# Where the spread reciprocals of a linear attention lie, how they are written, and when their transfers are issued

## The chip, the cores and the metric

The kernel runs on one core of one Trainium2 chip. The metric is device time in microseconds (us) of one execution. A NeuronCore has the engines TensorE (PE: matmuls; its weight loads are listed apart as PEld), VectorE (DVE), ScalarE (ACT), GpSimd (POOL) and SyncE (SP, which here only issues DMAs). All times of day below are us from the start of the profiled span.

## What is computed

Four layers in turn on x of 2048 tokens by 576 features: linear attention (A), MLP (B), A, B, each with a layer norm before it and a residual after it.

```python
def _A_ref(x, wqkv, wo):            # H = 32 heads of Dh = 18
    ...
    pq, pk = phi(q), phi(k)
    kv = jnp.einsum("bhsd,bhse->bhde", pk, v)
    z = jnp.einsum("bhsd->bhd", pk)
    num = jnp.einsum("bhqd,bhde->bhqe", pq, kv)
    den = jnp.einsum("bhqd,bhd->bhq", pq, z)[..., None] + 1e-6
    o = num / den
    return (lambda x, *d: x.transpose(*d))(o, 0, 2, 1, 3).reshape(B, S, D) @ wo
def _B_ref(x, w1, b1, w2, b2):      # F = 4608
    y = _layernorm(x, axis=-1)
    h = _gelu(jnp.einsum("bsd,df->bsf", y, w1) + b1)
    return jnp.einsum("bsf,fd->bsd", h, w2) + b2
```

The change concerns the division by `den`: one value per head and token.

## The kernel before

The 2048 tokens are cut into 16 tiles of 128 and into 4 blocks of 512, counted 0 to 3 here as in the code (the change's title counts them from 1). `yT` holds the normed activations with features on partitions: 128 partitions x 5 feature chunks x 2048 tokens, so block `c` has the columns `c * 512` to `(c + 1) * 512`. The heads lie in five groups `g` of 7, 7, 7, 7 and 4 heads. Work is written out by hand: `pe`, `vec`, `act`, `pool` and `sp` keep each engine's instructions in the order of the program (L45 to L63), SP's DMAs too. Waits between engines come from the tiles that they read and write.

An attention layer (`layer_A`, L467) first runs over the tiles for keys and values, then forms `kvwo`, the product of each head's key-value matrix with the output weights, so that a tile's output is one chain of five matmuls on `pq`, the query features. `pq` lies in slots of `units`; group 4 of two blocks (0 and 1, or 2 and 3) shares one slot, block `c` in the partitions from `64 * (c % 2)` on (L534 to L536, `q_rows` L652). A matmul of group 4 reads all 128 partitions of that slot.

Before the outputs, `pq` is divided by the denominators. For each block:

- `den_stage(c)` (L661): 24 small matmuls on PE give the denominators as 128 partitions (32 heads x 4 tiles) x 128 tokens; DVE takes the reciprocal into `rden`. For blocks 1 to 3 SP writes it to `rden_rows[c]` in DRAM, 32 heads x 512 tokens, in four DMAs of 32 rows, one per tile (L672).
- `spread(c)` (L678): 7 DMAs read `rden_rows[c]` back with each head's row repeated 18 times, so that each partition of `pq` has its head's reciprocals beside it. They go into `spare(0)` to `spare(4)`, the five chunks of `yT` in block 1's columns, whichever block they are for. Groups 0 to 3 take one DMA each (126 partitions), a fifth fills partitions 126 and 127 for all four, two more serve group 4.
- `scales(c)` (L789): five multiplies on DVE, one per group, `pq = spare * pq`.
- `outputs(c)` (L798): `wo_stage` for the block's 4 tiles, ten matmuls each on PE, and the residual on DVE.

Block 0 goes another way (`quad_rden`, `scale_first`): its reciprocals are spread by matmuls. In between, `groups(n)` (L793) lets PE do `n` of the next MLP's first-matmul groups on block 0, which need nothing of this. The layer ends with (L802 to L815):

```python
            scales(1)
            groups(3)
            den_stage(2)
            den_stage(3)
            outputs(1)
            spread(2)
            scales(2)
            spread(3)
            scales(3)
            groups(3)
            outputs(2)
            outputs(3)
```

`outputs(1)` stands ahead of `spread(2)` in the program, but puts nothing on SP here: a residual is followed by a DMA in the last layer alone (L464). Since `spread(2)` and `spread(3)` write the same rows, each waits until DVE's multiplies have read the earlier block's. The columns of `yT` for blocks 1 to 3 are filled anew, with the MLP's normed rows, only while the MLP runs (`place_rows`, L396).

Of the kernel before, what the change touches and what calls it, by code (L numbers as in the profile page):

```python
# [8 lines left out]
ALU = mybir.AluOpType  # L9
# [5 lines left out]
S, D, F, H, DH = 2048, 576, 4608, 32, 18  # L15
P = 128
# [11 lines left out]
TPC = CB // P  # L28
CA = 512
# [6 lines left out]
def build(tc, A_x, A_wqkv, A_wo, B_w1, B_b1, B_w2, B_b2, out, n_layers=4):  # L36
    nc = tc.nc
    with ExitStack() as ctx:
# [23 lines left out]
        vec, act = InOrder(nc.vector, "VectorE"), InOrder(nc.scalar, "ScalarE")  # L62
        pool, sp = InOrder(nc.gpsimd, "GpSimd"), InOrder(nc.sync, "SyncE")  # L63
# [21 lines left out]
        def one(name, tag=None):  # L85
            return ps_one.tile([P, 512], F32, name=name, tag=tag or one_tag())
# [106 lines left out]
        yT = const.tile([P, KD, S], BF16, name="yT")  # L193
# [16 lines left out]
        rden_rows = [dpool.tile([H, CA], BF16, name=f"rden_rows{c}") for c in range(NCA)]  # L210
# [12 lines left out]
        def mm(out_, lhsT, rhs, start, stop, **kw):  # L223
            return pe(nc.tensor.matmul(out_, lhsT=lhsT, rhs=rhs, start=start, stop=stop, **kw))  # L224
# [242 lines left out]
        def layer_A(li, next_kind, begin, before_tile, before_keys, mid_tile, rows_ahead, after_tile, q_tiles, placed, mlp):  # L467
            es, pks, kps, vas, pq, ys = {}, {}, {}, {}, {}, {}
# [183 lines left out]
            def q_rows(g, c):  # L652
                return slice(64 * (c % 2), 64 * (c % 2) + 64) if g == 4 else slice(0, P)

            def spare(i):

                return yT[:, i, CA:2 * CA]

            quad_rden = spare(3)

            def den_stage(c):  # L661
                dp = one("den_ps", "one3" if c == 0 else None)
                for g in range(G + 1):
                    for j in range(TPC):
                        sel, by = (zsel[:, g + (g == 4 and c % 2), :], pq[(g, c)][:, j * P:(j + 1) * P]) if g < G else (eps_sel[:], ident[:])
                        mm(dp[32 * j:32 * (j + 1), 0:P], sel, by, g == 0, g == G)
                rden = work.tile([P, P], BF16, name="rden", bufs=2)
                with nc.allow_low_precision("reciprocal of the denominator in the reference's bfloat16"):
                    vec.reciprocal(out=rden[:], in_=dp[:, 0:P])
                if c > 0:  # L670

                    for j in range(TPC):  # L672
                        sp.dma_start(out=rden_rows[c][:, j * P:(j + 1) * P], in_=rden[32 * j:32 * (j + 1), :])
                    return
                vec.tensor_tensor(out=quad_rden.rearrange("p (j n) -> p j n", j=4), in0=quad_mask[:],
                                  in1=rden[:].unsqueeze(1).to_broadcast([P, 4, P]), op=ALU.mult)

            def spread(c):  # L678
                heads = rden_rows[c]
                for g in range(4):  # L680
                    sp.dma_start(out=spare(g)[0:126, :],
                                 in_=heads[7 * g:7 * g + 7, :].unsqueeze(1).to_broadcast([7, DH, CA]))
                sp.dma_start(out=yT[126:P, 0:4, CA:2 * CA],
                             in_=heads[31:32, :].unsqueeze(1).to_broadcast([2, 4, CA]))
                at = 64 * (c % 2)
                sp.dma_start(out=spare(4)[at:at + 54, :], in_=heads[28:31, :].unsqueeze(1).to_broadcast([3, DH, CA]))
                sp.dma_start(out=spare(4)[at + 54:at + 64, :], in_=heads[31:32, :].to_broadcast([10, CA]))

            def scale_stage(g, c):
                rows = q_rows(g, c)  # L690
                vec.tensor_tensor(out=pq[(g, c)][rows, :], in0=spare(g)[rows, :], in1=pq[(g, c)][rows, :], op=ALU.mult)

            def scale_first(half, tags):

# [9 lines left out]
            def wo_stage(t):  # L704
                c, j = divmod(t, TPC)
                wp = pair("wo_ps")
                for half in range(2):
                    for g in range(G):
                        by = kvwo[g] if g < 4 else kvwo[g][c % 2]
                        mm(wp[:, half, 0:HALF], pq[(g, c)][:, j * P:(j + 1) * P],  # L710
                           by[:, half * HALF:(half + 1) * HALF], g == 0, g == G - 1)
                residual(li, t, wp[:, :, 0:HALF])
# [7 lines left out]
                              in1=side[0:126, 0:260].rearrange("p (g c) -> p g c", g=4)[:, :, 64:65].to_broadcast([126, 4, H]),  # L720
                              op=ALU.mult)
            vec.tensor_copy(out=products[0:65, 4, 0:V4].rearrange("p (g d) -> p g d", g=4), in_=tp[0:65, :, 0:126])
            vec.tensor_copy(out=zk[96:P, :].rearrange("p (i c) -> p i c", i=2),
                            in_=side[96:P, 264:328].unsqueeze(1).to_broadcast([32, 2, 64]))
# [3 lines left out]
                                     in1=sums_sb[96:P, :], op0=ALU.mult, op1=ALU.add)  # L728
            vec.tensor_tensor(
                out=kvT[0:72, 4, 0:72].rearrange("p (h e) -> p h e", h=4),  # L730
                in0=side[0:72, 264:336].rearrange("p (h e) -> p h e", h=4),
                in1=maskz[0:72, 0:4, :], op=ALU.mult)
# [3 lines left out]
            for k in range(KD):  # L736
                rows = slice(0, P if k < 4 else 65)
                for g in range(4):
# [5 lines left out]
                              in1=zp[:, 0:1].unsqueeze(1).to_broadcast([P, 2, H]), op=ALU.mult)  # L744
            vec.tensor_tensor(
                out=kvT[0:126, 0:4, :].rearrange("p g (h e) -> p g h e", h=7),
                in0=kvp[0:126, 0:V4].rearrange("p (g h e) -> p g h e", g=4, h=7),
                in1=maskz[0:126, :, :].unsqueeze(1).to_broadcast([126, 4, 7, DH]), op=ALU.mult)
            kv_wo(4, act)
            q_next(True, "one0")  # L750
            finish(len(q_late) - 3)
            den_stage(0)
            kv_wo(0, act)
            kv_wo(1, act)
# [26 lines left out]
            q_next(True)  # L781
            first[3].transposed()
            den_stage(1)
            spread(1)
            warm_table(ACT.Gelu_apprx_tanh)
            assert not q_left


            def scales(c):  # L789
                for g in range(G):  # L790
                    scale_stage(g, c)
# [6 lines left out]
            def outputs(c):  # L798
                for t in range(c * TPC, (c + 1) * TPC):
                    wo_stage(t)  # L800

            finish(len(q_late))  # L802
            scales(1)
            groups(3)
            den_stage(2)
            den_stage(3)
            outputs(1)
            spread(2)
            scales(2)
            spread(3)  # L810
            scales(3)
            groups(3)
            outputs(2)
# [216 lines left out]
        for li, kind in enumerate(kinds):  # L1030
            nk = kinds[li + 1] if li + 1 < n_layers else None
            if kind == "A" and li == 0:
                layer_A(li, nk, begin0, before_tile0, before_keys0, mid_tile0, rows_ahead0, after_tile0, (1, 2, 3, 5, 7, 10, NT - 2), False,
                        mlps.get(li + 1))
            elif kind == "A":
                layer_A(li, nk, None, lambda t: lnq.tick(), nothing, nothing, nothing, lambda *a: None, range(4, 10), True,
                        mlps.get(li + 1))
            else:
                mlps[li].run()
# [48 lines left out]
```

## Time and profile before

| | |
|---|---|
| median of 3 runs | 757.26 us (755.1 to 758.77) |
| the profiled execution | 757.15 us, its span 755.4 us |
| TensorE busy | 745.9 us, 99% of the span |
| VectorE, ScalarE, GpSimd busy | 36%, 39%, 15% |
| mean granted TensorE clock | 0.998 |
| DMA | 34.48 MB; the SP and ACT hardware queue (q1) takes 16.9% of 16 engines |
| `rden_rows<-rden` | 24 DMAs of 8 KB, issue 412 ns (median) |
| `yT<-rden_rows` | 42 DMAs, 24 of 126 KB, 6 of 54, 6 of 10 and 6 of 8; issue 729 ns (median) |

How to read a profile row: `L224 PE MATMUL wo_ps<-shared,units ... x288 | 42.8, 294 | 3.7 <-DVE units` means 288 matmuls recorded on line 224 (the helper `mm`) that write `wo_ps`, 42.8 us busy, 294 ns each, and 3.7 us in which the engine stood idle just before one of them, ended by DVE's write of `units`. L53 is the helper that issues every DVE, ACT, POOL and SP instruction, so these are told apart by their tiles. In the chain of work that ended last, "issue" is time with no visible wait, and "SPq" is SP issuing a DMA; a row "DMA" runs from the start of a transfer's issue to its landing. "PEclk" or granted clock is the share of full speed that TensorE's clock was allowed.

### The profile page before, as it was taken

How to read it: one execution, taken by the hardware profiler on the slowest of the kernel's cores; microseconds unless marked ns; L12 is line 12 of the kernel's file. 1: busy time of each engine (PE TensorE's matmuls, PEld its weight loads, DVE VectorE, ACT ScalarE, POOL GpSimd, SP SyncE). 2: the span in 40 equal slices, each digit the busy share in tenths (PEclk: the TensorE clock that was granted, in tenths of full speed). 3: DMA queues.
4: the chain of work that ended last, by engine and by line, in shares of the span. 5: the costliest groups of instructions: out<-in, count | busy, mean ns of one | idle time of the engine just before them, and what ended most of it. 6: DMA issues, size and time to landing. Idle time of an engine off the chain costs nothing.

```text
span 755.4 us, 15366 instructions
## 1 busy us (share of the span) xinstructions
PE 745.9 (99%) x6423; PEld 469.2 (62%) x6438; DVE 268.5 (36%) x653; ACT 298.1 (39%) x652; POOL 114.5 (15%) x245
## 2 busy tenths in 40 slices
PE   9999989999999999999999999999999999999998
PEld 5666446774477457646776665557646754774476
DVE  7987644333223402500355576333310240100000
ACT  5656841205700750274035475440174037205700
POOL 4541100321111201200200020012210120010010
PEclk9999999999999999999999999999999999999999
DMA  7990120022011202110032001102000200020000
GB/s 206 270 355 20 35 68 1 2 56 46 2 18 42 44 2 36 37 32 1 18 109 67 2 10 42 60 1 39 29 2 1 51 17 1 11 49 10 1 9 25
DMA packets 60741, 34.48 MB, mean 46 GB/s; under 512 B 37088, under 2 KB 60672, under 8 KB 60672
## 3 DMA queue, kind: packets, MB, share of 16 engines
q1 hardware_dynamic: 59312, 32.94, 16.9%
q8 instruction: 50, 0.82, 0.5%
q10 hardware_dynamic: 1360, 0.56, 0.3%
q14 instruction: 19, 0.16, 0.1%
HBM read 21.70 MB, written 4.93 MB: 35 GB/s over the span
## 4 chain that ended last, share of the span: by engine, by line
PE 92%; DMA 2%; SPq 2%; DVE 2%; issue 1%; POOL 0%; ACT 0%; DVEq 0%
PE m_ps L224 37%; PE hp_ps L224 19%; PE h_ps L224 15%; PE k_ps L224 6%; PE q_ps L224 5%; PE wo_ps L224 4%; PE rk_ps L224 3%; SPq L53 2%; DMA yT<-rden_rows 1%; DVE units L53 1%; PE tp L383 1%; PE side_ps L224 1%; DMA wkv_sb<-in_A_wqkv_dram 1%; PE den_ps L224 0%; PE kvwo_ps L224 0%
## 5 line engine op out<-in xcount | busy, mean ns | idle before, releaser
L224 PEld LDWEIGHTS <-units 128*128 128x128 bf16 x2688 | 260.8, 98 | 79.6 <-issue 5.1
L224 PE MATMUL m_ps<-w_sb,units 128*128 128x288 bf16 (+2 forms) x2304 | 283.6, 286 | 0.0
L224 PEld LDWEIGHTS <-w_sb 64*128 64x128 bf16 x2304 | 123.9, 94 | 136.7 <-ACT relay_sb L53 4.1
L224 PE MATMUL h_ps<-yT,w_sb 64*128 64x512 bf16 x1152 | 178.0, 376 | 0.0
L224 PE MATMUL hp_ps<-yT,w_sb 64*128 64x512 bf16 x1152 | 148.0, 376 | 0.1
L53 DVE TENSOR_TENSOR x_sb<-m_ps,xo 128x576 bf16<-128x576 f32 (+2 forms) x33 | 24.4, 738 | 325.3 <-PE m_ps L224 325.3
L53 ACT COPY relay_sb<-relay_sb 128x1 f32<-128x1 f32 x144 | 27.7, 192 | 270.4 <-PE hp_ps L224 253.7
L53 ACT ACTIVATE units<-hp_ps,b1T 128x512 bf16<-128x512 f32 x144 | 91.0, 683 | 59.1 <-PE hp_ps L224 58.2
L53 POOL TENSOR_TENSOR xo<-x_sb,b_bc 128x576 f32<-128x576 bf16 x32 | 40.7, 1273 | 414.0 <-DVE x_sb L53 299.4
L53 ACT ACTIVATE units<-h_ps,b1T 128x512 bf16<-128x512 f32 x144 | 96.1, 687 | 0.0
L224 PE MATMUL hp_ps<-yT,w_tail 64*128 64x512 bf16 x144 | 54.1, 376 | 0.0
L224 PE MATMUL h_ps<-yT,w_tail 64*128 64x512 bf16 x144 | 54.1, 376 | 0.0
L224 PE MATMUL k_ps<-wkv_sb,yT 128*128 128x288 bf16 (+1 forms) x320 | 52.5, 301 | 0.4 <-DMA wkv_sb<-in_A_wqkv_dram 0.2
L53 DVE BATCH_NORM_STATS2 ln_st<-x_sb 128x6 f32<-128x288 bf16 x128 | 51.3, 440 | 1.0 <-DMA x_sb<-in_A_x_dram 0.7
L53 ACT ACTIVATE phi_e<-k_ps 128x288 bf16<-128x288 f32 x64 | 26.4, 413 | 52.1 <-PE k_ps L224 50.8
L53 ACT ACTIVATE units<-q_ps 128x512 bf16<-128x512 f32 x72 | 38.4, 596 | 21.4 <-PE q_ps L224 21.2
L53 DVE STREAM_TRANSPOSE shared<-y_ring 128x640 bf16<-128x640 bf16 x40 | 32.9, 826 | 39.0 <-DMA yT<-shared 30.2
L224 PE MATMUL wo_ps<-shared,units 128*128 128x288 bf16 x288 | 42.8, 294 | 3.7 <-DVE units L53 3.7
L53 DVE TENSOR_SCALAR y_ring<-x_sb,ln_mv,ln_rstd 128x576 bf16<-128x576 bf16 x57 | 30.9, 542 | 41.4 <-POOL ln_rstd L53 41.4
L224 PE MATMUL q_ps<-yT,wq_sb 128*128 128x512 bf16 (+1 forms) x185 | 43.1, 380 | 0.7
L224 PEld LDWEIGHTS <-w_tail 64*128 64x128 bf16 x288 | 27.1, 94 | 17.0
L224 PEld LDWEIGHTS <-yT 128*128 128x128 bf16 x320 | 30.4, 98 | 11.2 <-issue 0.9
(96 smaller groups left out, 425.7 us busy)
## 6 DMA issues: line engine op xcount, KB each, us to landing
yT<-shared SPq DMA_DIRECT2D x160, 40.0 KB
w_sb<-in_B_w_dram SPq DMA_DIRECT2D x12, 432.0 KB
w_sb<-in_B_w_dram SPq DMA_DIRECT2D x9, 512.0 KB
yT<-rden_rows SPq DMA_DIRECT2D x24, 126.0 KB
y_rows<-y_ring SPq DMA_DIRECT2D x16, 144.0 KB
units<-y_rows SPq DMA_DIRECT2D x16, 144.0 KB
x_sb<-in_A_x_dram SPq DMA_DIRECT2D x15, 144.0 KB
out_dram<-x_sb SPq DMA_DIRECT2D x15, 144.0 KB
```

Source lines behind the costliest of these rows:

```text
L53: inst = issue(*args, **kw)
L224: return pe(nc.tensor.matmul(out_, lhsT=lhsT, rhs=rhs, start=start, stop=stop, **kw))
L383: pe(nc.tensor.transpose(out=tp[:, k - a, :], in_=self.y[:, k * P:(k + 1) * P], identity=ident[:]))
```

## The change

Three things change. (1) `spare(c)` is now block `c`'s own columns of `yT`, so that each block's spread reciprocals have a place of their own. (2) Each block's reciprocals are written to `rden_rows[c]` in one DMA that covers all 128 partitions (seen from DRAM as 4 tiles x 32 heads x 128 tokens) in place of four. (3) `spread(2)` and `spread(3)` stand right behind `den_stage(3)`, ahead of `outputs(1)`. `quad_rden` keeps the place that it had.

```diff
-            def spare(i):
-
-                return yT[:, i, CA:2 * CA]
-
-            quad_rden = spare(3)
+            def spare(c):
+
+                return yT[:, :, c * CA:(c + 1) * CA]
+
+            quad_rden = spare(1)[:, 3, :]
...
-                    for j in range(TPC):
-                        sp.dma_start(out=rden_rows[c][:, j * P:(j + 1) * P], in_=rden[32 * j:32 * (j + 1), :])
+                    sp.dma_start(out=rden_rows[c].rearrange("h (j n) -> j h n", j=TPC), in_=rden[:])
...
             def spread(c):
-                heads = rden_rows[c]
+                heads, to = rden_rows[c], spare(c)
+                at = 64 * (c % 2)
                 for g in range(4):
-                    sp.dma_start(out=spare(g)[0:126, :],
-                                 in_=heads[7 * g:7 * g + 7, :].unsqueeze(1).to_broadcast([7, DH, CA]))
-                sp.dma_start(out=yT[126:P, 0:4, CA:2 * CA],
-                             in_=heads[31:32, :].unsqueeze(1).to_broadcast([2, 4, CA]))
-                at = 64 * (c % 2)
-                sp.dma_start(out=spare(4)[at:at + 54, :], in_=heads[28:31, :].unsqueeze(1).to_broadcast([3, DH, CA]))
-                sp.dma_start(out=spare(4)[at + 54:at + 64, :], in_=heads[31:32, :].to_broadcast([10, CA]))
+                    sp.dma_start(out=to[0:126, g, :], in_=heads[7 * g:7 * g + 7, :].unsqueeze(1).to_broadcast([7, DH, CA]))
+                sp.dma_start(out=to[126:P, 0:4, :], in_=heads[31:32, :].unsqueeze(1).to_broadcast([2, 4, CA]))
+                sp.dma_start(out=to[at:at + 54, 4, :], in_=heads[28:31, :].unsqueeze(1).to_broadcast([3, DH, CA]))
+                sp.dma_start(out=to[at + 54:at + 64, 4, :], in_=heads[31:32, :].to_broadcast([10, CA]))

             def scale_stage(g, c):
                 rows = q_rows(g, c)
-                vec.tensor_tensor(out=pq[(g, c)][rows, :], in0=spare(g)[rows, :], in1=pq[(g, c)][rows, :], op=ALU.mult)
+                vec.tensor_tensor(out=pq[(g, c)][rows, :], in0=spare(c)[rows, g, :], in1=pq[(g, c)][rows, :], op=ALU.mult)
...
             den_stage(3)
+            spread(2)
+            spread(3)
             outputs(1)
-            spread(2)
             scales(2)
-            spread(3)
             scales(3)
```

## The prediction

> **What bounds the kernel now.** I read the page first, then the waits, then the two stretches where TensorE waits, then the clock in them. TensorE (PE) is busy nearly all the time, so only what lets it stand still or slows its clock can be won. On the page:
>
> ```profile
> PE 745.9 (99%) x6423; PEld 469.2 (62%) x6438; DVE 268.5 (36%) x653; ACT 298.1 (39%) x652; POOL 114.5 (15%) x245
> ...
> L224 PE MATMUL wo_ps<-shared,units 128*128 128x288 bf16 x288 | 42.8, 294 | 3.7 <-DVE units L53 3.7
> ```
>
> The last column is idle time ahead of a group. This group, the output projection, has 3.7 us of it; no other group of matmuls after the start has more than 0.7 us. The waits say how it is divided and what VectorE (DVE) in turn waited for:
>
> ```profile
> DVE units L53 <- DMA yT<-rden_rows: 24.4, 6, 5.0
> ...
> PE wo_ps L224 <- DVE units L53: 3.7, 2, 2.1
> ```
>
> Two waits, one in each attention layer. The timeline of the first:
>
> ```profile
> 110.73 0.66 PE L224 MATMUL wo_ps<-shared,units 128*128 128x288 bf16 x4
> 111.12 1.27 ACT L53 ACTIVATE units<-h_ps,b1T 128x512 bf16<-128x512 f32 x2
> 111.59 1.88 DVE L53 TENSOR_TENSOR units<-yT,units 128x512 bf16<-128x512 bf16 x5 [4.95 <-DMA yT<-rden_rows]
> 113.53 10.85 PEld L224 LDWEIGHTS <-units 128*128 128x128 bf16 x76 [2.44 <-DVE units L53]
> 113.53 6.75 PE L224 MATMUL wo_ps<-shared,units 128*128 128x288 bf16 x40 [2.14 <-DVE units L53]
> ```
>
> PE does the first four matmuls of `outputs(2)` (head groups 0 to 3 of block 2) at 110.73, then stands from 111.39 to 113.53. The fifth reads head group 4, and by L534 to L536 blocks 2 and 3 share one slot of `units` for it, so the last multiply of `scales(3)` must be done too. That is the end of the five DVE multiplies that start at 111.59, which waited for the DMAs of `spread(3)`. The second layer has the same picture with 1.54 us (482.91 to 484.45).
>
> Why `spread(3)` is late shows in the chain that ended last, followed in this stretch (start, us, what):
>
> ```profile
> 98.75 0.83 SPq L53
> ...
> 101.95 2.83 DMA yT<-rden_rows
> ...
> 104.88 0.86 DVE units L53 x3
> 105.74 0.15 issue
> 105.89 0.76 DVE units L53 x2
> 106.65 0.28 SPq L53
> ...
> 108.63 2.87 DMA yT<-rden_rows
> ```
>
> `spread(2)` is issued from 98.75 on, lands, is multiplied in by DVE from 104.88 on, and only then may `spread(3)` overwrite the same rows of `yT` (block 1's columns). Two round trips stand one behind the other.
>
> The second loss is the clock. The stretches' table (stretch, length, then busy us of PE, PEld, DVE, ACT, POOL, then granted clock, DMA share, GB/s):
>
> ```profile
> 111.40:113.50 2.10, 0.00 (x0) 0.00 (x0) 1.85 (x5) 0.99 (x2) 0.00 (x0) 1.00 0.03 9
> 113.50:114.90 1.40, 1.37 (x12) 1.10 (x13) 0.42 (x1) 0.00 (x0) 0.00 (x0) 1.00 0.00 0
> 114.90:118.30 3.40, 3.40 (x17) 2.17 (x15) 1.09 (x2) 0.00 (x0) 0.00 (x0) 0.50 0.02 5
> 118.30:122.00 3.70, 3.70 (x32) 2.96 (x31) 2.27 (x3) 0.00 (x0) 0.00 (x0) 1.00 0.00 0
> ```
>
> For 3.4 us after the first stall PE ran at half clock. The cost is checked by the chain: the same 76 `wo_ps` matmuls take 11.15 us in the first layer (113.53 on) and 9.48 us in the second (484.45 on), where the clock stayed at 1.00. The difference is 1.67 us.
>
> **The change, part by part.** The instruction order of PE, DVE, ACT and POOL stays as it is; only SP's queue and the places written change.
>
> *One transfer for each block's reciprocals.* Three blocks in two layers lose 3 SP issues each (18 in all), of 0.41 us (`rden_rows<-rden`, median 412 ns). SP's timeline around the stall:
>
> ```profile
> 82.33 1.70 SPq L53 DMA_DIRECT2D rden_rows<-rden  x4
> 85.13 5.14 SPq L53 DMA_DIRECT2D yT<-rden_rows  x7
> 94.73 3.85 SPq L53 DMA_DIRECT2D rden_rows<-rden  x8
> 98.75 11.61 SPq L53 DMA_DIRECT2D yT<-rden_rows  x14
> ```
>
> The eight writes of blocks 2 and 3 hold SP from 94.73 to 98.58, and `spread(2)` follows at once. With one write for each block the limit is the landing instead. For block 1 the last small write starts at about 83.61 (82.33 + 1.70 - 0.42) and `spread(1)` can start at 85.13, so a write of 32 rows takes 1.5 us from issue to being readable. No row shows one of 128 rows of 256 B viewed as 4 x 32. Below, it costs what the small one does, 1.5 us; less would help nothing, since SP first has block 3's write to issue, from 95.53 (block 3's reciprocal) to about 95.95. Above, the nearest row is `units<-y_rows`, the same 4 x 32 shape with rows of 1,152 B: its first 12 issues take 14.91 us at a DMA share of 0.25 to 0.29, about 1.24 us each, and its issue is up to 0.23 us longer at the median (639 against 412 ns): 1.5 + 1.24 + 0.23 = 3.0 us. I take 2.1 us, nearer the lower end, because the bytes are fewer (32 against 144 KB). Then `spread(2)` starts at 94.73 + 2.1 = 96.8 (96.2 to 97.7) in place of 98.75. `spread(1)` starts at 84.4 (83.8 to 85.3) in place of 85.13; PE doesn't wait for it now, and 0.2 us late it still wouldn't (`scales(1)` ends at 93.52, its reader starts at 93.96).
>
> [...]
>
> *Own columns, both spreads ahead.* `spread(3)` no longer waits for `scales(2)`. The columns of blocks 2 and 3 were last read by the query projections, which end by 79.4, so the new places bring no wait that matters. Each spread is 7 issues in 5.14 us (85.13). So `spread(3)` starts at 96.8 + 5.14 = 101.9 and its last issue at about 106.6 (5.14 less the last one's 0.45). The two landings of the chain, 2.83 and 2.87 us (3.05 in the second layer), put the last data at 109.7 at worst. DVE does `outputs(1)`'s residuals until 99.84, `scales(2)` from about 103, and `scales(3)` from 108 to 109.7 + 0.43 (one multiply) = 110.1. PE needs it at 111.39: 1.3 us to spare, 0.4 us with the slow write. Second layer: reciprocal done at 466.23, first write at 466.25, `spread(2)` from 468.35, last data at 481.2, multiply done at 481.7, PE needs it at 482.91: 1.2 us to spare. Both stalls go whole.
>
> What they are moved past: `outputs(1)` puts nothing on SP in these layers (L464), and SP holds only these DMAs here (its next work, `yT<-shared`, begins at 149.7). The spreads overlap each other more, but their engines keep up: a spread's 576 KB (4 x 126, 54, 10 and 8 on the page) at the 143 to 152 GB/s of 101 to 103 us is 4.0 us, less than SP's 5.1. PE and DMA meet nowhere else. What is late next: nothing within 0.4 us; `wo_ps` continues as in `outputs(1)`, whose 40 matmuls run from 93.96 with no wait.
>
> *The clock.* The granted clock is 1.00 everywhere but at the ends and in these 3.4 us (mean 0.998), and it follows the longest wait of PE in the span. Without the stall I expect no drop: 1.67 us.
>
> [...]
>
> **Sum.** The profiled run took 757.15 us (span 755.4 and 1.75 around it), 0.1 under the median of 757.26. 757.15 - 2.14 - 1.54 - 1.67 = 751.8 us, 0.7% less.
>
> **Rivals.**
> - A, a stall remains. If an issue of the spreads takes more than 0.86 us on average (13 of them between 96.8 and 108.0, the last start that still meets 111.39 with 2.9 + 0.43 us behind it), PE waits. At 0.95 us the last multiply ends at 96.8 + 12.35 + 2.9 + 0.43 = 112.5, a stall of 1.1 us, and by the same sum 1.1 in the second layer, too short for a clock drop: 757.15 - 1.04 - 0.44 - 1.67 = 754.0. Rows: 0.73 median for the large ones, up to 0.93.
> - B, the clock drops all the same, the stall not being its cause: 751.8 + 1.67 = 753.5. For it: the three runs span 755.1 to 758.77, wider than one drop. Against it: one drop in the span, and it begins 1.4 us after the longest wait of PE; outside these two waits and the start, PE's own row has no wait over 0.4 us.
> - C, slower. With no pause between them, 14 spreads back up on their engines, as `units<-y_rows` does, at 1.24 us an issue. From 1.03 us on the change loses in the first layer (2.14 us later than 0.86 allows). At 1.24 the last multiply ends at 96.8 + 13 x 1.24 + 2.9 + 0.43 = 116.2, a stall of 4.9; in the second layer also 4.9; with a drop of the clock in each: 757.15 + 2.7 + 3.4 + 1.67 = 765. Against it: 4.0 us of transfer against 5.1 of issue; `units<-y_rows` moves 144 KB at 97 GB/s, 1.5 us, against 0.64 of issue.
> - D, no effect: `spread(2)` or `(3)` still starts where it did, held by something the trace of before hides behind the wait for DVE: 757.
>
> **How the numbers follow.** Forecast 0.74 (own range 751.0 to 752.8: the margin of the sizes read), A 0.10, B 0.07, C 0.05, D 0.04. The range is to hold forecast, B and the better part of A: 750.8 to 754.2. A measurement can tell about 0.5% (3.8 us) from no change; under 753.4 is faster: the forecast, half of A and a third of B, 0.81; within: 0.14; slower: C, 0.05.
>
> **What would show it.** No wait of PE `wo_ps` on DVE `units`; the 76 `wo_ps` matmuls of `outputs(2)` and `(3)` at 9.5 us in both layers with clock 1.00; `spread(3)`'s first issue near 102 in place of 105.3; `scales(3)` done before 110.7. Wrong if the new write takes over 3.5 us to be readable, if the 14 issues take over 11 us, or if half clock shows elsewhere.

## The result and the profile after

The changed kernel takes 751.73 us (median of 6 runs, 751.48 to 751.83) against 755.61 us (median of 6, 754.65 to 758.77) before: a ratio of 0.9941, with a 95% interval of 0.9922 to 0.996. The three runs of before that were known at the prediction had a median of 757.26; three more, at 754.65, 754.97 and 756.11, brought it down. The profiled execution took 751.68 us with a span of 750.0, against 757.15 and 755.4: 5.4 us of span less.

On the page, the idle time ahead of the output projection is gone and its matmuls are at 286 ns in the mean (294 before):

```profile
PE 744.4 (99%) x6423; PEld 468.9 (63%) x6438; DVE 268.5 (36%) x653; ACT 298.3 (40%) x652; POOL 114.8 (15%) x245
...
L224 PE MATMUL wo_ps<-shared,units 128*128 128x288 bf16 x288 | 40.7, 286 | 0.0
```

SP's part of the timeline in the first attention layer, to be laid beside the four lines shown before:

```profile
82.50 0.63 SPq L53 DMA_DIRECT2D rden_rows<-rden  x1
84.65 4.98 SPq L53 DMA_DIRECT2D yT<-rden_rows  x7
94.90 1.36 SPq L53 DMA_DIRECT2D rden_rows<-rden  x2
97.06 10.75 SPq L53 DMA_DIRECT2D yT<-rden_rows  x14
```

Two writes in place of eight, and the 14 spread DMAs from 97.06 in place of 98.75. VectorE's part, where the five-fold rows are `scales(2)` and `scales(3)`:

```profile
103.27 1.76 DVE L53 TENSOR_TENSOR units<-yT,units 128x512 bf16<-128x512 bf16 x5 [3.27 <-DMA yT<-rden_rows]
109.06 1.88 DVE L53 TENSOR_TENSOR units<-yT,units 128x512 bf16<-128x512 bf16 x5 [4.04 <-DMA yT<-rden_rows]
```

The last multiply ends at 110.94 (113.47 before). TensorE, in the timeline and in the table of stretches:

```profile
110.58 0.38 PE L224 MATMUL h_ps<-yT,w_tail 64*128 64x512 bf16 x1
110.89 3.36 PE L224 MATMUL wo_ps<-shared,units 128*128 128x288 bf16 x26
```

```profile
111.40:113.50 2.10, 2.10 (x20) 1.68 (x18) 0.76 (x1) 1.16 (x2) 0.00 (x0) 1.00 0.00 0
113.50:114.90 1.40, 1.40 (x14) 1.13 (x12) 0.88 (x2) 0.00 (x0) 0.00 (x0) 1.00 0.05 12
114.90:118.30 3.40, 3.40 (x30) 2.71 (x29) 2.15 (x3) 0.00 (x0) 0.00 (x0) 1.00 0.00 0
```

Where it stood from 111.40 to 113.50 and ran at half clock from 114.90 to 118.30, it is now busy throughout at clock 1.00. The last of these stretches has 30 matmuls where it had 17. The chain that ended last no longer leaves TensorE in this part of the layer:

```profile
110.09 0.87 PE h_ps L224 x9
110.96 9.91 PE wo_ps L224 x80
120.87 1.18 PE hp_ps L224 x9
```

The two stalls (2.14 and 1.54) and the half clock (1.67) make 5.35 of the 5.4 us by which the span is shorter.

### The profile page after: what moved, and what is told of

It is laid out like the page before. It is cut to its first block, busy times and chain, and to the rows that moved or that the text cites. A ratio compares the mean times of both kernels' runs of the same rounds, so it can differ in the third digit from the quotient of the medians.

```text
span 750.0 us, 15346 instructions
## 1 busy us (share of the span) xinstructions
PE 744.4 (99%) x6423; PEld 468.9 (63%) x6438; DVE 268.5 (36%) x653; ACT 298.3 (40%) x652; POOL 114.8 (15%) x245
## 4 chain that ended last, share of the span: by engine, by line
PE 98%; DVE 1%; DMA 0%; issue 0%; POOL 0%; ACT 0%; DVEq 0%
PE m_ps L224 38%; PE hp_ps L224 21%; PE h_ps L224 17%; PE k_ps L224 6%; PE wo_ps L224 5%; PE q_ps L224 5%; PE rk_ps L224 3%; PE tp L383 1%; PE side_ps L224 1%; PE den_ps L224 0%; DVE ln_st L53 0%; PE kvwo_ps L224 0%; PE rden_ps L224 0%; PE kv_ps L224 0%; DMA x_sb<-in_A_x_dram 0%
## 5 line engine op out<-in xcount | busy, mean ns | idle before, releaser
L224 PE MATMUL wo_ps<-shared,units 128*128 128x288 bf16 x288 | 40.7, 286 | 0.0
```

## Experiments

My theory: only two things cost time, TensorE's wait for the last multiply of `scales(3)` and a half clock that such a wait can bring. Rivals: that the transfers cost TensorE time in some other way; that own columns alone, or the single write alone, carry the gain; and that the half clock has nothing to do with the stall. One part needed no run: with `outputs(1)` put back ahead of the two spreads in the program, every engine's list of instructions and waits is the same as in the changed kernel. So the third part of the change, the order in the source, does nothing; what lets `spread(3)` go early is its own place.

### The kernel before again

No edit.

> The kernel of before once more, for the granted clock of each of its executions. Theory (the clock drop is caused by the stall, and comes or not with where the stall falls): executions fall into steps of about 1.7 us that go with the mean clock: 1.000 at about 755.4, 0.998 at about 757.1, 0.995 at about 758.8 (757.15 - 1.67 for one drop less, + 1.67 for one more). Rival (the drop has nothing to do with the stall): the kernel after shows drops as often as this one, and times here don't go with the clock.

Measured: 755.3 us (median of 12, 754.63 to 759.34), ratio to before 1.0001 (0.9988 to 1.0014). Together with the 22 runs of before on the same chip there are 34 executions with their mean clock. 23 are at 1.000, with a median of 755.06 us (754.41 to 756.95); 2 at 0.999; 8 at 0.998, with a median of 756.75; one at 0.995, at 759.34. The steps of about 1.7 us between 1.000 and 0.998 are there, so the half clock came in about one execution in four. The no-drop executions are also shorter than the 755.4 I expected, and the profiled one shows why: its stalls are smaller, 1.52 and 1.35 us, 2.9 in sum (3.7 in the profile shown ahead of the prediction):

```profile
PE wo_ps L224 <- DVE units L53: 2.9, 2, 1.5
```

So the typical gain is the stalls alone, about 3.3 us (755.06 to 751.73), and the profile shown ahead of the prediction came from one of the longer executions.

### Own columns, four writes

```diff
-                    sp.dma_start(out=rden_rows[c].rearrange("h (j n) -> j h n", j=TPC), in_=rden[:])
+                    for j in range(TPC):
+                        sp.dma_start(out=rden_rows[c][:, j * P:(j + 1) * P], in_=rden[32 * j:32 * (j + 1), :])
```

> The kernel after, but with four small writes for each block's reciprocals. Theory (only the lateness of the last multiply counts): spread(2) starts at 98.75 as before, the last multiply ends 13.9 us (first attention layer) and 12.9 us (second) after that as in the kernel after, at 112.6 and 482.9, against 111.39 and 482.91 when TensorE wants it: stalls of 1.2 and 0 us, no clock drop, 752.9 us (751.7 to 753.2). Rival (the single write carries no weight): 751.7.

Measured: 753.39 us (752.98 to 754.63, 10 runs), ratio to before 0.9969 (0.9958 to 0.9981), clock 1.000 in all. The waits of its profile and its timeline in the first layer:

```profile
PE wo_ps L224 <- DVE units L53: 1.6, 2, 1.2
```

```profile
112.69 3.48 PE L224 MATMUL wo_ps<-shared,units 128*128 128x288 bf16 x27 [1.25 <-DVE units L53]
```

The stall of the first layer is 1.25 us (1.2 expected), that of the second 0.40 (0 expected). The single write does carry weight: without it the spreads start at 98.82, where they did before, and the last multiply ends 1.3 us too late.

### One write, old columns

The single write (the line with a minus above) put into the kernel before.

> The kernel before with the single write alone: block 1's columns for all, spread(3) behind the multiplies of block 2. Theory: spread(2) starts 1.85 us earlier (94.73 + 2.16 in place of 98.75) in the first attention layer and 1.57 us earlier in the second, and all behind it too; the last multiply ends at 111.6 and 482.8, against 111.39 and 482.91: stalls of 0.2 and 0 us, 751.9 us (751.6 to 752.6), so one part alone does nearly all. Rival (two round trips behind one another are the cause, and only own columns end them): the stalls stay over 1 us in both layers, 754 us or more.

Measured: 752.64 us (752.2 to 753.47, 5 runs), ratio to before 0.9961 (0.9946 to 0.9976), clock 1.000 in all. In its profiled execution (753.45 us) the second layer has no stall, as expected, but the first has 1.46 us and not 0.2. The chain shows what I had left out, a slow landing:

```profile
105.49 0.73 SPq L53
...
106.32 0.72 SPq L53
107.04 0.05 issue
107.09 4.05 DMA yT<-rden_rows
```

`spread(3)`'s fifth DMA took 4.05 us from issue to landing, where the rows of before had 2.5 to 3.05. It fills partitions 126 and 127, which the first of the five multiplies reads, so all five wait for it. Three of the other four runs are 0.8 to 1.25 us shorter than the profiled one, so the landing was probably faster there; none of them was profiled.

The records of this trace tell a little more. Of the completions of the second, third and fourth DMA of this spread, the last is recorded 1.1 us behind the one before it each time (109.33 against 108.19 us for the second). Just before, at 107.23, the instruction queue (q14) moved one packet of 8 KB that took 0.77 us. In the first layer of the other profiles such a packet took 0.34 to 0.55 us and the last completion of these DMAs lagged less than 0.4 us. Only the run with own columns and four writes had a longer packet, 1.06 us, and there the last completion of two DMAs lagged 1.0 us. Whether the packet delayed the transfers isn't shown: no run tried it, and lags of up to 0.7 us occur in second layers without such a packet.

Both theories are half right. Of the 3.3 us that the whole change gains, the single write alone gives 2.4 (755.06 to 752.64) and own columns alone 1.7 (755.06 to 753.39); of these three kernels only the one with both shows no stall in its profile. Even that one has little room: the same slow landing would stop TensorE for about 0.6 us. This is an estimate from the profile after, where the fifth DMA landed after 2.99 us and 0.43 us were to spare (4.05 - 2.99 - 0.43; the 0.43 is worked out further down).

### More cover

The kernel before with the same work in another order, DMAs and waits as they were:

```diff
-            groups(3)
+            groups(4)
             outputs(2)
             outputs(3)
-            groups(2)
+            groups(1)
```

> The kernel before, its DMAs and waits unchanged, with four groups of the MLP between the outputs of block 1 and those of block 2 in place of three, and one at the end in place of two: the same work. Theory (the loss is TensorE's wait and the clock drop behind it, nothing else): TensorE comes to outputs(2) 3.9 us later, at 115.3, after the last multiply at 113.5: no stall, no drop, 751.7 us. Rival (the transfers into block 1's columns, or SP's queue, cost TensorE time beside that wait): above 752.5.

Measured: 751.55 us (751.36 to 752.55, 5 runs), ratio to before 0.9947 (0.9933 to 0.9962). The waits of its profile have no line of `wo_ps` or of the weight loads for DVE's `units`, while the DMA waits are as long as before:

```profile
DVE units L53 <- DMA yT<-rden_rows: 23.2, 6, 4.8
```

With the transfers untouched and only TensorE's work moved in front of the wait, the time is that of the changed kernel to 0.2 us. The transfers cost TensorE nothing else that can be seen; the rival falls. The longest of the five runs, 752.55, is the profiled one; there TensorE waited 1.4 us at the start for the key and value weights (`wkv_sb`), long before the stretch that was reordered.

### The kernel after again

No edit.

> The kernel after once more, beside the next two on one chip. Theory (no stall, so no drop of the clock and nothing that varies): every execution at clock 1.000, between 751.4 and 752.0 us. Rival (the drop has nothing to do with the stall, and its absence so far is chance): about one execution in four at 0.998 and 1.7 us longer, as in the kernel before.

Measured: 751.57 us (751.32 to 754.08, 5 runs), ratio to before 0.9958 (0.9944 to 0.9972; 9 runs of before with a median of 754.81, all at 0.999 or 1.000). Four executions are at 0.999 or 1.000 between 751.32 and 751.96; one took 754.08 at clock 0.997. With the first six that is 1 of 11 with a half clock, so "every execution" was wrong. Where TensorE stood in that one isn't recorded. It is 2.6 us longer than the median of the other four, of which one half clock explains 1.7.

### Less cover, after and before

The kernel after, and the kernel before, with one group moved the other way:

```diff
-            groups(3)
+            groups(2)
             outputs(2)
             outputs(3)
-            groups(2)
+            groups(3)
```

> The kernel after with two groups of the MLP between the outputs of block 1 and those of block 2 in place of three, and three at the end in place of two: the same work, and TensorE wants the last multiply 3.89 us earlier, at 107.6 and 475.1 against its end at 110.9 and 477.5. Theory (lateness of the last multiply becomes TensorE's wait one to one, and a wait of over 2 us brings the half clock): stalls of 3.3 and 2.4 us, 751.7 + 5.7 = 757.4 us without a drop, and 1.7 more for each drop, most executions with one or two: 759 to 761 us at clock 0.998 to 0.995. [...]

> The kernel before with the same shift of one group. Stalls of 1.5 + 3.9 = 5.4 and 1.35 + 3.9 = 5.25 us (from the execution with clock 1.000). Theory: 755.1 + 7.8 = 762.9 us without a drop, and with one behind each stall 766.3 us at clock 0.995 in nearly every execution. Rival (drop not tied to the stall): 763 at 1.000 in most.

Measured, after: 760.55 us (759.46 to 761.31, 5 runs), ratio 1.0074 (1.006 to 1.0087), clock 0.998 once and 0.995 or 0.996 four times. Before: 767.15 us (766.88 to 767.37, 4 runs), ratio 1.0158 (1.0144 to 1.0172), clock 0.991 in all.

Lateness does become a stall one to one: 3.48 and 2.40 us in the profile after (3.3 and 2.4 expected), 5.62 and 5.35 in that of before (5.4 and 5.25 expected). And every one of these nine executions has the half clock, so these longer stalls brought it; the rival falls. The kernel before was to have clock 0.995 and 766.3 us; it came out at 0.991 and 767.15, as its clock is halved for 6.8 us at each stall and not for 3.4; TensorE stands through part of that. But the rule isn't the length of the stall. From the table of stretches of the kernel after, first the stall of 3.48 us and what follows it, then that of 2.40:

```profile
107.50:111.00 3.50, 0.06 (x1) 0.00 (x0) 1.85 (x5) 1.05 (x2) 0.00 (x0) 1.00 0.11 39
111.00:115.00 4.00, 3.96 (x33) 3.18 (x34) 2.08 (x3) 0.00 (x0) 0.00 (x0) 1.00 0.00 0
478.70:481.10 2.40, 0.05 (x1) 0.00 (x0) 1.85 (x5) 1.04 (x2) 0.00 (x0) 1.00 0.08 28
481.20:484.60 3.40, 3.40 (x15) 2.18 (x16) 0.76 (x1) 0.00 (x0) 0.00 (x0) 0.51 0.00 0
484.70:488.00 3.30, 3.30 (x29) 2.63 (x28) 2.08 (x3) 0.00 (x0) 0.00 (x0) 1.00 0.00 0
```

The longer stall leaves the clock at 1.00, the shorter one halves it. In the kernel before with less cover the clock falls while TensorE still stands:

```profile
107.70:110.20 2.50, 0.03 (x1) 0.00 (x0) 0.00 (x0) 1.02 (x2) 0.00 (x0) 1.00 0.42 143
110.20:113.30 3.10, 0.00 (x0) 0.00 (x0) 1.85 (x5) 0.00 (x0) 0.00 (x0) 0.50 0.13 41
113.40:117.00 3.60, 3.60 (x16) 2.28 (x17) 0.76 (x1) 0.00 (x0) 0.00 (x0) 0.50 0.00 0
117.00:121.00 4.00, 4.00 (x34) 3.21 (x33) 2.29 (x4) 0.00 (x0) 0.00 (x0) 1.00 0.00 0
```

What fits all of them is a grid of time steps, worked out from the trace's records of when the granted clock changed. In the profile of before these lie at 5.66, 114.89, 118.30 and 756.59 us. The last three are 32, 33 and 220 steps of 3.4133 us behind the first (750.93 / 220). In the kernel before with less cover the second drop begins 375.47 us after the first, 110 of these steps. The half clock lasted one step (114.89 to 118.30 in the profile of before, 481.25 to 484.66 in the kernel after with less cover) or two (110.21 to 117.03 in the kernel before with less cover).

Now the stalls can be divided by the steps:

- In the kernel after with less cover the grid has a mark at 109.19, 109 steps ahead of 481.25. It lies in the middle of the stall from 107.56 to 111.03, so that one falls into two steps, with 1.63 and 1.84 us idle, and there is no drop.
- In the same kernel the stall of 2.40 us lies within one step, and the clock is halved in the next.
- In the profile of before the stall from 111.39 to 113.53 has 2.06 us within the step that ends at 114.89, and the clock falls just there.

So in these traces a step with 1.84 us idle of 3.41 kept the clock and one with 2.06 lost it for the next step. The boundary between them wasn't tried further. The other profiles agree: their stalls have 1.46 us or less in any one step without a drop, and 2.48 us or more with one. If this holds in other executions too (an estimate from these traces, nothing more), a stall of about 2 us costs 1.7 us more or not, depending on where it falls on the grid. That would explain why the kernel before loses it in about one execution in four, but this isn't shown, since only one execution of it with a half clock was profiled. The one execution of the kernel after at clock 0.997 isn't explained: without the half clock it is 0.9 us longer than the others, and no stall of 1.54 us or less was followed by a drop in these traces.

## Why the prediction was right, point by point

- **Time: right.** 751.8 us forecast, 751.73 measured, within the range. The sum was made against one execution, and its three terms are 5.35 of the 5.4 us by which the two spans differ.
- **The single write: right, 2.1 us forecast, 2.16 measured** (94.90 to 97.06; 2.14 in the second layer, 462.45 to 464.59). The DMA view of the stretch around the write of block 1 has, for the four small writes before and then for the one after:

```profile
q1 hardware_dynamic: 192, 0.03, 5.8%
```

```profile
DMA  0000000000000000000000001222333331000000
...
q1 hardware_dynamic: 132, 0.03, 6.9%
```

  The first number of a q1 line is packets. By the sizes in the two traces, 128 packets are of 256 B in both cases; the others are of 4 B, 64 for the four small writes and 4 for the one. In flight the one write has a DMA share of 0.2 to 0.3 of 16 engines. The one write is readable some 0.7 us later after its issue than a small one (2.16 against 1.5 us), less than the three issues that it saves (3 x 0.41).
- **Both spreads ahead: right in kind, with less room than I worked out.** `spread(3)` starts at 102.76, forecast 101.9: the write is readable 0.3 us later, and SP pauses 0.53 us in `spread(2)`, with no wait that the trace shows. The last multiply ends at 110.94, forecast 110.1 at worst, and TensorE's fifth matmul follows the four of 0.12 us each that start at 110.89, so 0.43 us were to spare where I had 1.3. The second layer had about 1.4 (477.51 against 478.9), where I had 1.2. My worst case took the slowest landing seen (3.05 us), and the run with 4.05 shows that it was not the worst.
- **Rivals A, C and D: refuted by the profile after.** 14 issues took 10.75 and 10.23 us, not over 11, `spread(2)` starts 1.7 us earlier, and there is no stall and no backing up.
- **The clock: right for the execution profiled, mis-sized for the median.** The step "Without the stall I expect no drop: 1.67 us" took a loss that only about a quarter of the executions of before pay as part of every one. So the forecast of 0.7% became 0.6%: the forecast gain of 5.3 us holds for one execution against another, and the medians differ by 3.9. One execution of the kernel after in 11 had a half clock all the same; whether without a stall, as rival B has it, or behind one isn't known. As a rule rival B is refuted by the runs with less cover, where a longer stall brought the drop in all nine executions.
- **What the drop follows: right that it is a stall, but the length alone doesn't say which.** Drops followed stalls of 2.14 us (before) and 2.40 us (after with less cover), and none followed one of 3.48 us (after with less cover).
- **The order in the source** was priced as nothing that is moved past, and is nothing at all.

## What to carry to other kernels

When a kernel's bound engine waits for a chain of transfers, look for what makes the links wait on each other (a place written twice, a queue held by many small issues), and count the room that is left after the change against the slowest landing seen in any trace, not the mean; or move work that needs none of it in front of the wait, which here gave the same time by moving one group of matmuls. Before making a sum against one profiled execution, look at how the runs spread: a loss can be in some executions and not in others, as the half clock was here in about one of four of the kernel before (9 of 34), and a median then won't give back all of it. An order in the source that crosses no instruction of the same engine is no change.

## What the runs showed of the hardware that was not expected

In these traces TensorE's half clock followed stalls of 2.14 and 2.40 us but not one of 3.48 us; its edges lie on a grid of 3.4133 us (750.93 / 220 in the profile of before), and it followed 2.06 us idle within one step and not 1.84. The landing of a spread's fifth DMA (8 KB) took 4.05 us once, where its like took 2.5 to 3.05 in the profile of before and 2.2 to 3.3 in all the others. That landing came behind a packet of the instruction queue that took 0.77 us; whether this is the cause isn't shown. The stall of one and the same program also varies from one execution to the next, by 0.6 us between the two that were profiled (2.14 against 1.52 us in the first layer of the kernel before).
